# A token-mixing and channel-mixing kernel: ScalarE copies the first block product, and one more query block is computed with seven products

## The chip, the cores and the metric

One core of a Trainium2 chip runs the whole program. TensorE multiplies matrices into PSUM, VectorE and ScalarE do elementwise work and are the ones that read PSUM, GpSimd and SyncE mostly issue DMAs. The engines run side by side and meet through semaphores; each takes its instructions in the order in which the program lists them. The metric is the device time of one execution in microseconds (us).

## The reference

For each of 8 batches, with S = 3008 rows and D = 256 columns:

```python
scores = (1.0 / S) * np.matmul(z, z.transpose(0, 2, 1))
x = u * np.matmul(np.maximum(scores, 0.0) ** 2, v)
xt = x.transpose(0, 2, 1)
h = np.maximum(xt @ w_tok1, 0.0) @ w_tok2
u2 = x + h.transpose(0, 2, 1)
h2 = np.maximum(u2 @ w_ch1, 0.0) @ w_ch2
out = u2 + h2
```

`z` has 64 columns, `w_tok1` is 3008 x 256, `w_ch1` is 256 x 1536 and `w_ch2` is 1536 x 256.

## The kernel before, in words

**Tiling.** A batch is cut into six query blocks of 512 rows (the last has 448), numbered q = 0 to 5; HALF is 3. A batch goes through attention for its six blocks (scores, relu, square, product with v), then the token mixing (`tok1`, `tok2`) and then, block by block, the channel mixing (`ch1`, then `product` or `ch2`). Channel mixing of blocks 3 to 5 of a batch is held back until attention of the next batch is over, so in the steady state TensorE alternates: about 68 us of attention of batch b+1 (267.27 to 335.15 us in the trace for batch 2), then blocks 3 to 5 of batch b together with the token mixing of batch b+1, then blocks 0 to 2 of batch b+1, then attention again. The point where attention ends and the held-back blocks begin is called the handover below.

**Order of work.** The kernel is built by a planner in Python. It keeps an estimated time for each engine, and lists of pieces for TensorE (`heads`, `tails`) with a cost, a list of events that they need and, behind them, operations for ScalarE, VectorE and SyncE (`push`) with a ready time and an estimated duration. It writes the instructions of all engines in the order that it comes to. Once built, the order is fixed.

**Attention's end.** For each of the two column halves of a block, `finish` (L809 on) has ScalarE copy one PSUM bank of the accumulator to a tile `cp` (L825), VectorE adds the other bank (L831) and `gate` multiplies by u into `xT` (L851, and L856 for the last 64 rows). The `cp` tiles come from the pool tag `res`, which has three buffers and is shared with the tiles `u_sb`, which hold a block of u2 until its output is written.

**Channel mixing, first half.** The hidden layer has twelve tiles of 128; `ch1` makes two of them at a time (four matmuls of 512 columns at L1192 into a pair of banks `hp`), and ScalarE, or VectorE where the planner finds ScalarE too busy, evacuates them through a relu (L1231) into `h2pre`. For blocks that are `grouped`, the first four of the twelve tiles (a third) are made another way, as a two by two block product with seven multiplications in place of eight, after Strassen and Winograd. Its seven products are issued in four stages "a" to "d" (`grouped_ch1`, L1312, tile `gp`), of four, four, four and two matmuls of 256 columns. Three sums of inputs (`t_sums`, L1268 to L1278) come first. Between the stages ScalarE copies results within and out of PSUM: after stage a it keeps a copy (L1323) and then forks one bank into the other (L1320); after b it applies a relu (L1327) and forks again; after c VectorE adds both banks with the kept copy (L1338); after d a last relu (L1331). Stage b waits for the first fork, c for the second, d for the two-bank add.

**Channel mixing, second half.** `h2pre @ w_ch2` is also a seven-product block product, for 47 of the 48 blocks. `make_sums` has VectorE form sums of `h2pre` (`hsum`, L1383, L1388, L1401); `product` (L1447) issues the products k = 1 to 7, twelve matmuls of 128 columns each (six for q = 5); `collect` (L1480) has VectorE add each product from PSUM into the output tile `ro`. Products 1, 6, 7, 4 go to the first bank of a pair `xb`, product 2 to the first bank of a pair `zb` and 5 and 3 to its second. VectorE reads product 1 for one quarter of the output, and product 6 then goes on accumulating on top of it in the same bank; product 2 is added to the same quarter by VectorE.

**Orders by hand.** `GROUPED`, `ORDER_LAST` and a plain tuple give, for each block, the order in which its seven products are listed with the pieces of the next block between them: a digit 1 to 7 is a product, 0 is a `ch1` piece of the next block (or a `ch2` piece of the last one), a letter is a stage of the next block's grouped product. `GROUPED` is used where the next block is grouped.

Of the kernel before, what the change touches and what calls it, by code (L numbers as in the profile page):

```python
# [9 lines left out]
F32 = mybir.dt.float32  # L10
BF16 = mybir.dt.bfloat16
# [3 lines left out]
P = 128  # L15
QW = 512
# [42 lines left out]
def kernel(  # L59
# [11 lines left out]
    nc = tc.nc  # L71
    B, S, D = u.shape
# [948 lines left out]

    hid_done = Done()
    BORROW = 3
    GROUPED = ("a", 0, 1, 2, "b", 6, 5, 0, "c", 7, 3, 0, 4, "d")
    VERY_LAST = (B - 1, NQ - 1, CHT // 2 - 1)
    ORDER_LAST = ((1, 2, 6, 5, 7, 0, 3, 4), (1, 2, 6, 5, 0, 7, 3, 0, 4))

    def add_mixer(b):
        st = {}
# [149 lines left out]
        def ch1(q, c2, borrowed, end):  # L1179
            slots = [take_slot()[0] for _ in range(1 + ((b, q, c2) == VERY_LAST))]  # L1180
            W = widths[q]
            xT = xTs[b, q]
            if c2 % 2 == 0:
                live["h2"] += 1
                st["h2", q, c2 // 2] = sb.tile(
                    [P, 4, QW], BF16, tag="h2", name="h2pre", bufs=ROOM["h2"])
            hps = [bank_pair(slot, "hp") for slot in slots]
            hp = hps[0]
            for r in range(2):
                cc = 2 * c2 + r  # L1190
                for dc in range(DT):
                    nc.tensor.matmul(  # L1192
                        hps[r % len(hps)][:, r, :W], w_ch1_sb[:, dc, cc * P:(cc + 1) * P],
                        xT[:, dc, :W], start=(dc == 0), stop=(dc == DT - 1))
# [12 lines left out]

            if (b, q, c2) == VERY_LAST:
                landed, freed = [], Done()

                def evacuate_part(r, t):
                    if r:
                        nc.scalar.activation(h2[:, r, :W], hps[1][:, r, :W], ACT.Relu)
                    else:
                        nc.vector.tensor_single_scalar(h2[:, r, :W], hp[:, r, :W], 0.0, AX.max)
                    landed.append(t)
                    if len(landed) == 2:
                        h2_done[q, c2].t = freed.t = max(landed)
                        keep_ends()

                for r, engine, at, busy in ((0, "dve", end - 0.18, 0.62), (1, "act", end + 0.21, 0.5)):
                    push(engine, at, busy, busy + 0.16, lambda t, r=r: evacuate_part(r, t))
                ring.extend((freed, slot) for slot in slots)
                release("xT", xT_uses[q])
                return
            on_act = load("act") + 0.92 < load("dve") + 2.15

            def evacuate(t):
                recent[0] = h2[:, 0, :1]
                if on_act:  # L1230
                    nc.scalar.activation(h2[:, :, :W], hp[:, :, :W], ACT.Relu)  # L1231
# [22 lines left out]
        g_done = {(q, d, k): Done() for q in range(NQ) for d in range(CHT // 4) for k in range(3)}  # L1254

        def token_quarters(q):

            xT = xTs[b, q]
            quarter = xT.rearrange("p k (m n) -> p k m n", m=2)
            tile_ = {}  # L1260

            def first_two(t):
                live["xT"] += 2
                tile_["T"] = sb.tile(
                    [P, 4, 2 * P], BF16, tag="xT", name="t_sums", bufs=ROOM["xT"])
                st["T", q] = tile_["T"]
                st["s5", q] = sb.tile([P, QW], F32, tag="xT", name="s5", bufs=ROOM["xT"])
# [12 lines left out]
            def begin(t):  # L1280
                push("dve", t, 0.4, 0.53, first_two, room=lambda: live["xT"] < ROOM["xT"] - 1)

            if u_done[q].t is None:
                st["want", q] = begin
            else:
                begin(max(pe[0], u_done[q].t))

        def grouped_ch1(q, d, stage, end):
# [41 lines left out]
            def relu_last(t):  # L1330
                nc.scalar.activation(h[:, 1, 0], half(1), ACT.Relu)  # L1331
                recent[0] = h[:, 1, 0, :1]
                live["xT"] -= 2
                if ("rest", q, d) in st:
                    st.pop(("rest", q, d))(t)

# [77 lines left out]

        def bank_of(q, k):

            if k in (2, 5, 3):
                return st["zb", q][:, int(k != 2)]
            return st["xb", q][:, 0]

        def product(q, k, end):

# [5 lines left out]
            if k == 2:  # L1428
# [28 lines left out]
        def collect(q, k, end):  # L1457
# [9 lines left out]
            def us(m, h):  # L1467
                return st["u", q][:, h, m * n:m * n + n, :]

            blocks_of = {1: (0, 0), 2: (0, 0), 5: (1, 1), 6: (1, 0), 3: (1, 0), 7: (1, 1),  # L1470
                         4: (0, 1)}
            opening = k in (1, 5, 6, 4)

            def add(t):
                if k == 1:
# [26 lines left out]
            if k == 4:  # L1502
                ring.append((done, st["x_slot", q]))

        over = [7] * NQ
# [135 lines left out]
        def add_product(q, k):  # L1641
            needs = {
                1: [Sooner(h2_done[q, c], 0.111 * c) for c in range(CHT // 2)] + w_done[2:],
                2: [], 5: [mix_done, taken[q, 2]], 6: [taken[q, 1]], 3: [taken[q, 5]], 7: [taken[q, 6]],
                4: [taken[q, 7]]}[k]
            kind = {5: 0, 7: 1, 6: 2, 4: 3}.get(k)
            if kind is not None:
                needs = needs + [Sooner(s_done[q, d, kind], 0.222 * d) for d in range(CHT // 4)]
            if q == NQ - 1 and k == 5 and b % 2 == 0:
                needs = needs + [tok1_over[b + 1]]  # L1650
            cost = pairs_of(q) * (CHT // 2) * column_time(P)
            tails.append(Piece(cost, needs, lambda end: product(q, k, end), opens=k == 1,
                               closes=k == 4, key=(b, 2 + q), slot=k in (1, 2),
                               joins=k == 1 and q == NQ - 1))

        added = [0] * (NQ + 1)
# [6 lines left out]
        for q in range(NQ):  # L1663
# [5 lines left out]
            if fast(q):  # L1669
                us_uses[q][0] += bool(rest)  # L1670
                h2_uses[q] += bool(rest)
                for k in (ORDER_LAST[b % 2] if q == NQ - 1 else GROUPED if grouped(q + 1) else
                          (0, 0, 1, 2, 0, 6, 5, 0, 7, 3, 0, 4)):
# [416 lines left out]
```

## Time and profile before

| | us |
|---|---|
| median of 3 runs | 1109.5 (1109.03 to 1110.85) |
| the profiled execution, its own time | 1109.13 |
| its span, first to last instruction | 1107.3 |
| TensorE busy | 1102.2 |
| VectorE busy | 811.5 |
| ScalarE busy | 684.7 |

The granted TensorE clock was full throughout. In lines of the timeline the first number is the start in us from the span's beginning, the second the time from the first start to the last end of the merged instructions, then engine, source line, operation, output and inputs with shapes, and the count; in brackets stands the idle time of the engine just before and what ended it. In lines of groups, the numbers behind the bar are the busy time in us and the mean of one in ns. Lines of waits read: who waited, for whom, us in total, how often, the longest. PEld is TensorE's weight load.

### The profile page before, as it was taken

Reading aid. Unit: us, or ns where it says so; the run is one execution under the profiler, and the core shown is the slowest. Engines: PE = TensorE matmul, PEld = TensorE weight load, DVE = VectorE, ACT = ScalarE, POOL = GpSimd, SP = SyncE. Lnnn points to the kernel's source line nnn. Section 1 sums busy time; section 2 is a strip of 40 time slices with the busy share of each in tenths; the row PEclk is TensorE's granted clock in tenths of the full one; section 3 lists DMA queues with packets and bytes.
Section 4 is the critical chain, followed back from the end, with each engine's and each line's share of the span. In section 5 each row is a group of like instructions: output and inputs, shape, how many; then the busy total and the mean of one; then the engine's idle time right before and its main releaser. Section 6 shows DMA issues by size and latency. Waiting matters only on the chain.

```text
span 1107.3 us, 27459 instructions
## 1 busy us (share of the span) xinstructions
PE 1102.2 (100%) x11199; PEld 695.2 (63%) x11199; DVE 811.5 (73%) x1791; ACT 684.7 (62%) x906; POOL 168.2 (15%) x386
## 2 busy tenths in 40 slices
PE   9999999999999999999999999999999999999998
PEld 3444575776557665576656865557755677556776
DVE  6889865886758866578766796567966778656785
ACT  7999555646854567546665467663776537743464
POOL 5320110321003110032100320003210120000100
PEclk9999999999999999999999999999999999999999
DMA  9999947798978969789896796977989778684222
GB/s 179 167 199 184 149 96 152 127 179 146 190 127 149 190 133 177 127 156 191 140 189 120 133 218 141 170 122 150 198 160 169 116 145 185 125 160 104 64 59 96
DMA packets 465726, 165.55 MB, mean 150 GB/s; under 512 B 433024, under 2 KB 448960, under 8 KB 465600
## 3 DMA queue, kind: packets, MB, share of 16 engines
q1 hardware_dynamic: 436208, 131.11, 58.9%
q0 software_dynamic: 28880, 32.32, 21.5%
q8 instruction: 87, 1.43, 0.6%
q14 instruction: 39, 0.32, 0.1%
q10 hardware_dynamic: 512, 0.38, 0.1%
HBM read 65.40 MB, written 24.64 MB: 81 GB/s over the span
## 4 chain that ended last, share of the span: by engine, by line
PE 99%; DVE 0%; ACT 0%; issue 0%
PE acc L697 42%; PE hp L1192 19%; PE xb L1447 11%; PE zb L1447 8%; PE sc L470 6%; PE h_ps L1128 4%; PE a_ps L1058 3%; PE gp L1312 3%; PE op L1544 2%; PE first_acc L614 1%; PE wp L210 0%; DVE at L516 0%; ACT at L508 0%; DVE zr L183 0%; PE first_acc L189 0%; DVE zT L1850 0%
## 5 line engine op out<-in xcount | busy, mean ns | idle before, releaser
L697 PEld LDWEIGHTS <-v_sb 64*128 64x128 bf16 x4418 | 245.7, 94 | 212.5 <-issue 1.3
L1231 ACT ACTIVATE h2pre<-hp 128x1024 bf16<-128x1024 f32 (+1 forms) x245 | 239.9, 1005 | 182.7 <-PE hp L1192 180.5
L697 PE MATMUL acc<-at,v_sb 64*128 64x512 bf16 (+1 forms) x2738 | 341.6, 374 | 0.0
L508 ACT ACTIVATE at<-sc 128x1024 bf16<-128x1024 f32 (+1 forms) x290 | 286.8, 1027 | 72.0 <-PE sc L470 66.4
L516 DVE TENSOR_TENSOR at<-at 128x1024 bf16<-128x1024 bf16 (+1 forms) x290 | 198.1, 687 | 112.1 <-ACT at L508 107.9
L1192 PE MATMUL hp<-xT,w_ch_sb 128*128 128x512 bf16 (+1 forms) x984 | 238.3, 374 | 0.0
L697 PE MATMUL acc<-fl,v_sb 64*128 64x512 bf16 (+1 forms) x1680 | 193.0, 367 | 0.0
L1192 PEld LDWEIGHTS <-w_ch_sb 128*128 128x128 bf16 x984 | 90.8, 98 | 79.0 <-issue 2.6
L1447 PEld LDWEIGHTS <-hsum 128*128 128x128 bf16 x2088 | 127.9, 98 | 19.6 <-issue 0.5
L470 PE MATMUL sc<-zT 64*128 64x512 bf16 (+1 forms) x732 | 132.4, 359 | 0.1
L1383 DVE TENSOR_TENSOR hsum<-h2pre 128x1024 bf16<-128x1024 bf16 (+1 forms) x141 | 90.0, 647 | 22.7 <-ACT h2pre L1231 12.6
L825 ACT COPY cp<-acc 128x512 f32<-128x512 f32 (+1 forms) x94 | 54.9, 584 | 79.9 <-PE acc L697 69.0
L831 DVE TENSOR_TENSOR cp<-acc,cp 128x512 f32<-128x512 f32 (+1 forms) x94 | 63.4, 675 | 54.8 <-ACT cp L825 54.0
L1447 PEld LDWEIGHTS <-h2pre 128*128 128x128 bf16 x1566 | 93.8, 98 | 10.0
L496 ACT ACTIVATE at<-sc 128x512 bf16<-128x512 f32 (+3 forms) x152 | 56.2, 450 | 29.2 <-PE sc L470 28.8
L1447 PE MATMUL xb<-shared_sb,hsum 128*128 128x128 bf16 x1044 | 73.6, 219 | 0.0
L1480 DVE TENSOR_TENSOR ro<-xb,u_sb 128x256 f32<-128x256 f32 (+1 forms) x141 | 56.3, 400 | 17.9 <-PE xb L1447 17.7
L470 PEld LDWEIGHTS <-zT 64*128 64x128 bf16 x732 | 42.4, 94 | 41.6 <-issue 3.8
L129 POOL CAST mark<-at 128x1 f32<-128x1 bf16 x24 | 9.3, 386 | 388.1 <-DVE at L516 388.1
L851 DVE TENSOR_TENSOR xT<-cp,uT 128x512 bf16<-128x512 f32 (+1 forms) x94 | 62.4, 663 | 0.8
L547 DVE TENSOR_TENSOR at<-at 128x512 bf16<-128x512 bf16 (+3 forms) x152 | 41.0, 320 | 23.8 <-ACT at L496 23.8
L1401 DVE TENSOR_TENSOR hsum<-h2pre,hsum 128x512 bf16<-128x512 bf16 (+1 forms) x141 | 55.1, 400 | 4.1 <-ACT h2pre L1331 2.5
(107 smaller groups left out, 1114.8 us busy)
## 6 DMA issues: line engine op xcount, KB each, us to landing
out_dram<-ro SPq DMA_DIRECT2D x40, 512.0 KB, 3.2
v_sb<-in_v_dram POOLq DMA_DIRECT2D x40, 256.0 KB, 4.6
ur<-in_u_dram POOLq DMA_DIRECT2D x40, 256.0 KB, 5.0
w_tok_sb<-in_moe_w_tok_dram POOLq DMA_DIRECT2D x10, 256.0 KB, 10.5
shared_sb<-in_z_dram POOLq DMA_DIRECT2D x35, 64.0 KB, 4.2
at<-at SPq DMA_TRANSPOSE x114, 2.4
out_dram<-ro SPq DMA_DIRECT2D x7, 256.0 KB, 3.7
fl<-at SPq DMA_TRANSPOSE x105, 4.5
```

Source lines behind the costliest of these rows:

```text
L470: nc.tensor.matmul(sc[:, r, c0:c1], zT[h, k:k + P], zT[h, m + c0:m + c1], start=True, stop=True)
L496: nc.scalar.activation(a3[:, i, c0:c1], sc[:, r, c0:c1], ACT.Relu, scale=inv_S)
L508: nc.scalar.activation(view, sv, ACT.Relu, scale=inv_S)
L516: nc.vector.tensor_mul(view, view, view)
L697: nc.tensor.matmul(o, vs[blk.b, g][rows, i, dh * P:(dh + 1) * P], rhs, start=(dh, h) not in blk.begun, stop=stop, skip_group_check=True)
L831: nc.vector.tensor_add(cp[:, :W], acc[:, 0, :W], cp[:, :W])
L851: nc.vector.tensor_mul(xT[:, dh, :full * P].rearrange("p (t s) -> p t s", s=P), acc[:, :full * P].rearrange("p (t s) -> p t s", s=P), uT[: ...
L1192: nc.tensor.matmul(hps[r % len(hps)][:, r, :W], w_ch1_sb[:, dc, cc * P:(cc + 1) * P], xT[:, dc, :W], start=(dc == 0), stop=(dc == DT - 1))
L1231: nc.scalar.activation(h2[:, :, :W], hp[:, :, :W], ACT.Relu)
L1383: nc.vector.tensor_sub(sums["s"][:, 0:2, :, :n * P], h[:, :, 1], h[:, 0])
L1447: nc.tensor.matmul(to[:, i * P:(i + 1) * P], lhs, weights[:, c2, :], start=(first_use and c2 == 0 and i == 0), stop=(c2 == CHT // 2 - 1), ...
L1480: nc.vector.tensor_add(res(m, h), source, us(m, h) if opening else res(m, h))
```

## The change

1. After product 1, ScalarE copies the first bank of `xb` into the second one (`fork` in `collect`). Product 2 accumulates on that copy, and product 6 on the original. VectorE reads product 1 no more; it takes the quarter once, from the second bank, after product 2, so it does six adds for a block and not seven. Product 2 and product 6 now wait for the copy. `zb` holds 5 and 3 alone and is taken when product 5 comes.
2. Block q = 4 of batches 1 to 6 becomes `grouped` too. Its input sums are started when the fifth `ch1` piece of block 3 is issued (`LATE_T`), and its sums and kept copy live in a buffer of the tag `h2` and not `xT`.
3. The orders are other ones: `GROUPED` is a tuple of orders, by block and apart for the last batch, `PLAIN` is the order where the next block isn't grouped, and `ORDER_LAST` is changed. Products 1 and 2 no longer follow each other; a `ch1` piece, product 6 or a stage stands between.

In the order that is built, the fourth block (q = 3) of batches 1 to 6 begins, right at the handover, with stage a of block 4, product 1, a `ch1` piece and stage b. On ScalarE the copy of the last attention accumulator comes first, then the kept copy and fork of stage a, then the copy of product 1, then the evacuation of the `ch1` piece. In these batches one evacuation each has moved from ScalarE to VectorE.

```diff
-    GROUPED = ("a", 0, 1, 2, "b", 6, 5, 0, "c", 7, 3, 0, 4, "d")
+    LATE_T = 4
+    FIRST = 2
+    GROUPED = (('a', 0, 1, 0, 'b', 6, 2, 5, 'c', 7, 0, 3, 'd', 4), ('a', 0, 1, 0, 'b', 2, 6, 5, 'c', 7, 0, 3, 'd', 4), (0, 'a', 0, 1, 0, 'b', 2, 6, 5, 'c', 7, 0, 3, 'd', 4), ('a', 1, 0, 'b', 2, 5, 6, 'c', 0, 7, 3, 'd', 0, 4), ('a', 0, 1, 0, 'b', 6, 2, 5, 'c', 7, 0, 3, 4, 'd'), ('a', 0, 1, 0, 'b', 6, 2, 5, 'c', 7, 0, 3, 'd', 4), ('a', 0, 1, 0, 'b', 6, 2, 5, 'c', 7, 0, 3, 'd', 4))
+    PLAIN = (0, 1, 0, 5, 2, 6, 0, 0, 7, 3, 0, 4)
-    ORDER_LAST = ((1, 2, 6, 5, 7, 0, 3, 4), (1, 2, 6, 5, 0, 7, 3, 0, 4))
+    ORDER_LAST = ((1, 6, 2, 5, 7, 0, 3, 4), (1, 6, 2, 5, 7, 0, 3, 0, 4))
...
-            if c2 == (3 if q else 0) and q + 1 < NQ and grouped(q + 1):
+            if c2 == (0, 3, 3, LATE_T if b < B - 1 else 3)[min(q, HALF)] and q + 1 < NQ and grouped(q + 1):
                 token_quarters(q + 1)
...
-            return b > 0 and 0 < q <= HALF and d == 0
+            return b > 0 and 0 < q <= HALF + (b < B - 1) and d == 0
...
+                else:
+                    live["h2"] += 1
+                    kept = sb.tile([P, 2, QW], F32, tag="h2", name="t_s5", bufs=ROOM["h2"])
+                    tile_["T"] = kept[:, 0].bitcast(BF16).rearrange("p (k n) -> p k n", k=4)
+                    st["s5", q] = kept[:, 1]
...
-            if k in (2, 5, 3):
-                return st["zb", q][:, int(k != 2)]
-            return st["xb", q][:, 0]
+            if k in (5, 3):
+                return st["zb", q][:, 0]
+            return st["xb", q][:, int(k == 2)]
...
-            first_use = k in (1, 2, 5)
+            first_use = k in (1, 5)
...
+            def fork(t):
+                nc.scalar.copy(bank_of(q, 2)[:, :n * P], bank_of(q, 1)[:, :n * P])
...
             if k == 1:
+                push("act", ready, busy, busy + 0.15, fork, first=2, done=done)
+            elif k == FIRST:
                 with_u(q, ready, lambda at: push(
                     "dve", at, busy, busy + 0.15, add, first=1, room=(home_of(q),),
                     frees=frees_of(q), done=done))
...
-                2: [], 5: [mix_done, taken[q, 2]], 6: [taken[q, 1]], 3: [taken[q, 5]], 7: [taken[q, 6]],
-                4: [taken[q, 7]]}[k]
+                2: [taken[q, 1]], 5: [mix_done], 6: [taken[q, 1]], 3: [taken[q, 5]], 7: [taken[q, 6]],
+                4: [taken[q, 7], taken[q, 2]]}[k]
```

More of the change, by code (lines that the diff above doesn't have):

```diff
@@ L1245, in ch1, with in_xT @@
                 release("xT", xT_uses[q])
-            if c2 == (3 if q else 0) and q + 1 < NQ and grouped(q + 1):
+            if c2 == (0, 3, 3, LATE_T if b < B - 1 else 3)[min(q, HALF)] and q + 1 < NQ and grouped(q + 1):
                 token_quarters(q + 1)
         def grouped(q, d=0):
-            return b > 0 and 0 < q <= HALF and d == 0
+            return b > 0 and 0 < q <= HALF + (b < B - 1) and d == 0
         t_done = {q: Done() for q in range(NQ)}
         g_done = {(q, d, k): Done() for q in range(NQ) for d in range(CHT // 4) for k in range(3)}
+        def in_xT(q):
+            return q <= HALF or b == B - 1
         def token_quarters(q):
@@ L1262, in first_two @@
             def first_two(t):
-                live["xT"] += 2
-                tile_["T"] = sb.tile(
-                    [P, 4, 2 * P], BF16, tag="xT", name="t_sums", bufs=ROOM["xT"])
+                if in_xT(q):
+                    live["xT"] += 2
+                    tile_["T"] = sb.tile(
+                        [P, 4, 2 * P], BF16, tag="xT", name="t_sums", bufs=ROOM["xT"])
+                    st["s5", q] = sb.tile([P, QW], F32, tag="xT", name="s5", bufs=ROOM["xT"])
+                else:
[3 more added lines that the diff above has]
+                    st["s5", q] = kept[:, 1]
                 st["T", q] = tile_["T"]
-                st["s5", q] = sb.tile([P, QW], F32, tag="xT", name="s5", bufs=ROOM["xT"])
                 nc.vector.tensor_sub(tile_["T"][:, 0:2], quarter[:, :, 1], quarter[:, 0])
@@ L1280, in begin @@
             def begin(t):
-                push("dve", t, 0.4, 0.53, first_two, room=lambda: live["xT"] < ROOM["xT"] - 1)
+                push("dve", t, 0.4, 0.53, first_two,
+                     room=(lambda: live["xT"] < ROOM["xT"] - 1) if in_xT(q) else ("h2",))
             if u_done[q].t is None:
@@ L1332, in relu_last @@
                 recent[0] = h[:, 1, 0, :1]
-                live["xT"] -= 2
+                if in_xT(q):
+                    live["xT"] -= 2
+                else:
+                    live["h2"] -= 1
                 if ("rest", q, d) in st:
@@ L1427, in product @@
                 st["xb", q] = bank_pair(st["x_slot", q], "xb")
-            if k == 2:
+            if k == 5:
                 st["z_slot", q], _ = take_slot()
@@ L1468, in us @@
                 return st["u", q][:, h, m * n:m * n + n, :]
-            blocks_of = {1: (0, 0), 2: (0, 0), 5: (1, 1), 6: (1, 0), 3: (1, 0), 7: (1, 1),
-                         4: (0, 1)}
-            opening = k in (1, 5, 6, 4)
+            blocks_of = {2: (0, 0), 5: (1, 1), 6: (1, 0), 3: (1, 0), 7: (1, 1), 4: (0, 1)}
+            opening = k in (2, 5, 6, 4)
+            def fork(t):
+                nc.scalar.copy(bank_of(q, 2)[:, :n * P], bank_of(q, 1)[:, :n * P])
             def add(t):
-                if k == 1:
+                if k == FIRST:
                     home, n_home = take_home(q)
@@ L1503, in collect @@
                 ring.append((done, st["x_slot", q]))
-        over = [7] * NQ
+        over = [6] * NQ
         us_uses = [[1] for _ in range(NQ)]
@@ L1652, in add_product @@
             tails.append(Piece(cost, needs, lambda end: product(q, k, end), opens=k == 1,
-                               closes=k == 4, key=(b, 2 + q), slot=k in (1, 2),
+                               closes=k == 4, key=(b, 2 + q), slot=k in (1, 5),
                                joins=k == 1 and q == NQ - 1))
@@ L1671, in add_mixer @@
                 h2_uses[q] += bool(rest)
-                for k in (ORDER_LAST[b % 2] if q == NQ - 1 else GROUPED if grouped(q + 1) else
-                          (0, 0, 1, 2, 0, 6, 5, 0, 7, 3, 0, 4)):
+                for k in (ORDER_LAST[b % 2] if q == NQ - 1 else GROUPED[q + (b == B - 1) * (HALF + 1)] if grouped(q + 1) else
+                          PLAIN):
                     if isinstance(k, str):
```

## The prediction

> **What bounds the kernel now.** I read the page first, then who waited for whom on TensorE, then the timeline of one handover from attention to channel mixing, engine by engine. The page's first part, its chain, and TensorE's waits:
>
> ```profile
> PE 1102.2 (100%) x11199; PEld 695.2 (63%) x11199; DVE 811.5 (73%) x1791; ACT 684.7 (62%) x906; POOL 168.2 (15%) x386
> PE 99%; DVE 0%; ACT 0%; issue 0%
> PE wp L210 <- DVE zero L1735: 1.2, 1, 1.2
> PE first_acc L614 <- DVE at L516: 0.4, 1, 0.4
> ```
>
> The chain that ended last is TensorE for 99% of the span, and the only waits above 0.15 us on it are two at the start. Busy time alone would not prove a pace, because ends of matmuls are modelled; starts are not. TensorE at the handover of batch 1, where attention ends and mixing begins:
>
> ```profile
> 331.25 3.96 PE L697 MATMUL acc<-fl,v_sb 64*128 64x448 bf16 x40
> 335.15 2.76 PE L1192 MATMUL hp<-xT,w_ch_sb 128*128 128x512 bf16 x12
> 337.75 0.83 PE L1447 MATMUL xb<-w_ch_sb,h2pre 128*128 128x128 bf16 x12
> 338.42 0.83 PE L1447 MATMUL zb<-w_ch_sb,h2pre 128*128 128x128 bf16 x12
> 339.09 1.03 PE L1192 MATMUL hp<-xT,w_ch_sb 128*128 128x512 bf16 x4
> ```
>
> From start to start, twelve 512-column matmuls take 2.60 us (0.217 each), a product of twelve 128-column ones 0.67 us, and nothing lies between. So the time changes by what TensorE must issue, and by any wait that reaches it.
>
> The Trainium skill (Perfetto Trace Analysis, Identifying the Most-Contended Engine) says that matmul busy time is no measure of headroom and that the weight loads' busy share is one. By that share, 63% here, columns would be worth little and the saving below would be 0; the starts above speak for counting them in full, and I do.
>
> **Columns.** The fifth block of batches 1 to 6 swaps two channel pieces of four 512-column matmuls (8 x 0.217 = 1.73 us) for fourteen 256-column ones. The same form in an earlier block:
>
> ```profile
> 239.02 0.38 PE L1312 MATMUL gp<-xT,w_ch_sb 128*128 128x256 bf16 x2
> 239.24 0.38 PE L1312 MATMUL gp<-t_sums,shared_sb 128*128 128x256 bf16 x2
> 239.46 1.03 PE L1192 MATMUL hp<-xT,w_ch_sb 128*128 128x512 bf16 x4
> 240.32 0.83 PE L1447 MATMUL xb<-w_ch_sb,h2pre 128*128 128x128 bf16 x12
> ...
> 240.22 0.61 ACT L1323 COPY s<-gp 128x512 f32<-128x512 f32 x1
> 240.86 0.57 ACT L1320 COPY gp<-gp 128x512 f32<-128x512 f32 x1
> ```
>
> Two take 0.22 us, so fourteen take 1.54. Saved: 0.19 us a block, 6 blocks: **-1.2 us**. The products of the second channel matmul keep their number and columns.
>
> **Work on ScalarE and VectorE.** Forty-seven adds of product 1 on VectorE go and 47 copies on ScalarE come (40 of 256 columns, 7 of 128). The grouped fifth block adds, six times, three sums, one two-bank add, a kept copy, two forks and two relus, and removes two evacuations; six more evacuations move from ScalarE to VectorE.
>
> ```profile
> L1231 ACT ACTIVATE h2pre<-hp 128x1024 bf16<-128x1024 f32 x198 | 198.5, 1026 | 146.7 <-PE hp L1192 145.6 <-issue 1.1
> L1320 ACT COPY gp<-gp 128x512 f32<-128x512 f32 x42 | 23.9, 570 | 1.3
> L1078 ACT COPY a_f<-a_ps 128x128 f32<-128x128 f32 x8 | 2.1, 265 | 33.7 <-PE a_ps L1058 33.7
> L1480 DVE TENSOR_TENSOR ro<-xb,u_sb 128x256 f32<-128x256 f32 x120 | 50.3, 419 | 12.1 <-PE xb L1447 11.9
> ```
>
> No row has a copy of 256 columns from PSUM to PSUM. It lies between 265 and 570 ns; a third of the way, since 256 is a third of the way from 128 to 512, gives an estimate of 0.37 us. ScalarE gains about 40 x 0.37 + 7 x 0.27 = 16.7 us of forks, and the swap of five shorter operations (about 0.58 each) for three evacuations of 1.03 leaves it within 2 us. VectorE loses 47 x 0.42, at most 19.7 us, and gains about as much. Both stay under 75% of the span; these sums cost nothing as long as the queue order holds, which is the next question.
>
> **Does the fork make TensorE wait?** Product 2 (or 6) may start only when the fork is done. In the changed order 1.30 us of other work follows product 1 in grouped blocks (one channel piece 0.86, one pair of short matmuls 0.44), and at least 1.43 (0.76 + 0.67) in the others of full width. The chain is 0.20 us from TensorE to ScalarE (the piece started at 339.09 ends at 339.95, its evacuation starts at 340.15, below), 0.37 for the copy, 0.05 back: 0.62. Alone it is hidden with 0.7 us to spare, so 0 is taken; behind an evacuation that has just begun (0.92 more) it would be 1.54, which bounds the cost at 0.24 us in 27 grouped blocks and 0.11 in 13 plain ones, 7.9 us in all. From below 0 bounds it, since a wait that isn't there can't be removed.
>
> **Waits that go.** Product 6 used to wait for VectorE's add of product 1:
>
> ```profile
> 377.85 0.42 DVE L1480 TENSOR_TENSOR ro<-xb,u_sb 128x256 f32<-128x256 f32 x1
> 378.01 0.38 PE L1312 MATMUL gp<-t_sums,shared_sb 128*128 128x256 bf16 x2
> 378.32 0.83 PE L1447 MATMUL xb<-shared_sb,hsum 128*128 128x128 bf16 x12
> 1092.02 0.92 PE L1192 MATMUL hp<-xT,w_ch_sb 128*128 128x448 bf16 x4
> 1092.50 0.42 DVE L1480 TENSOR_TENSOR ro<-xb,u_sb 128x256 f32<-128x256 f32 x1
> 1092.97 0.83 PE L1447 MATMUL xb<-shared_sb,hsum 128*128 128x128 bf16 x12
> ```
>
> The pair at 378.01 needs 0.22 and the product starts 0.09 late, 0.05 after the add's end; the piece at 1092.02 needs 0.76, the product starts 0.19 late. Both go: **-0.3 us** (0 to -0.3).
>
> **The new wait: six handovers.** In the fourth block of batches 1 to 6 the order now starts with stage a, product 1, one channel piece, stage b. Stage b needs the kept copy and the first fork of stage a, and both stand on ScalarE behind the copy of the last attention accumulator (L825). That copy is late already:
>
> ```profile
> ACT cp L825 <- DVE xT L856: 10.7, 7, 1.7
> 198.34 4.49 PE L1192 MATMUL hp<-xT,w_ch_sb 128*128 128x512 bf16 x20
> 199.63 0.53 ACT L825 COPY cp<-acc 128x448 f32<-128x448 f32 x1 [0.60 <-DVE xT L856]
> ...
> 333.74 0.53 ACT L825 COPY cp<-acc 128x448 f32<-128x448 f32 x1 [1.25 <-PE acc L697]
> 336.01 0.53 ACT L825 COPY cp<-acc 128x448 f32<-128x448 f32 x1 [1.74 <-DVE xT L856]
> 336.44 1.03 ACT L1231 ACTIVATE h2pre<-hp 128x1024 bf16<-128x1024 f32 x1
> ...
> 340.15 1.02 ACT L1231 ACTIVATE h2pre<-hp 128x1024 bf16<-128x1024 f32 x1 [0.85 <-PE hp L1192]
> ...
> 331.55 0.69 DVE L516 TENSOR_TENSOR at<-at 128x1024 bf16<-128x1024 bf16 x1 [3.59 <-ACT at L508]
> 332.16 0.68 DVE L1383 TENSOR_TENSOR hsum<-h2pre 128x1024 bf16<-128x1024 bf16 x1
> 332.76 0.69 DVE L516 TENSOR_TENSOR at<-at 128x1024 bf16<-128x1024 bf16 x1
> 333.36 0.42 DVE L1388 TENSOR_TENSOR hsum<-h2pre,hsum 128x512 bf16<-128x512 bf16 x1
> ...
> 334.37 0.62 DVE L831 TENSOR_TENSOR cp<-acc,cp 128x448 f32<-128x448 f32 x1
> 334.90 0.42 DVE L926 TENSOR_TENSOR d_pair<-x_pair 128x512 bf16<-128x512 bf16 x1
> 335.24 0.55 DVE L851 TENSOR_TENSOR xT<-cp,uT 128x384 bf16<-128x384 f32 x1
> 335.71 0.22 DVE L856 TENSOR_TENSOR xT<-cp,uT 128x64 bf16<-128x64 f32 x1
> ```
>
> Call T the start of mixing, 335.15. The second accumulator's copy needs the buffer of the first, which VectorE frees with L856 at 335.93, so it starts at T+0.86 and the evacuation behind it at T+1.29, though its piece ended at 335.15 + 0.87 = 336.02, ready by 336.22. Before the change nobody needed that evacuation early.
>
> After it, VectorE's queue there reads: square, two sums of 1024, square, a sum of 512, L831, a sum of 512, L851, L856. With the steps above (0.61, 0.60, 0.60, 0.60, 0.34) from 331.55 it is free at T-0.85; the first copy ends at 334.27, so L831 starts at T-0.84, and 0.53 + 0.34 + 0.47 + 0.22 later L856 ends at T+0.72. The copy starts at T+0.80, the kept copy 0.43 later, at T+1.23, the fork 0.64 after that and ends at T+2.44; with 0.05 back stage b can start at T+2.49. TensorE gets there at T + 0.44 + 0.67 + 0.86 = T+1.97. It waits 0.52 us, six times: **+3.1 us**. Behind stage b on TensorE stand all later products, so the delay is not made up. Bounds: 0, if the buffer comes free in time; by the row at 199.63, T+1.29 in batch 0 with the start of mixing at 198.34, the copy is 0.49 later and the wait 1.01, or 6.1 us.
>
> The Trainium skill (PSUM — Partial Sum Buffer, Engine vs sequencer instructions) says that ScalarE's queue is strict first in, first out. By that rule the sum is as above; if the kept copy could pass the waiting one it would start at T+0.64, the fork would end at T+1.85, stage b would be on time and the sum would lack the 3.1. The evacuation held until 336.44 agrees with the rule.
>
> **The sum.** -1.2 - 0.3 + 3.1 = +1.6 us on the profiled execution's own 1109.13 us (span 1107.3, 1.8 around it): **1110.7 us**, 0.11% over the median of the runs shown, 1109.5.
>
> **Rivals.**
> *The handover is on time.* If L856 or the buffer rotation lets the copy start 0.5 us earlier, only -1.5 is left: 1107.6 us. For it speaks that TensorE has no such wait now; against it the seven waits for L856, at every handover.
> *The wait spreads at the handover.* After stage b an evacuation, relu and second fork follow on ScalarE before stage c, which TensorE reaches 2.01 us after b ends. Forks and relu of 0.6 each behind a 1.03 evacuation that starts after the product's fork, at about T+2.65, finish at T+4.9, where stage c is due at T+4.94: nothing to spare. If the copy is 0.3 later than worked out, both waits grow, 6 x (0.3 + 0.1), and the time is 1113.1 us: slower. It decides from a start of the copy at about T+1.0. The batch 0 row speaks for it, the five full steps of VectorE above against it.
> *The fork waits behind evacuations in all 47 blocks*: the 7.9 us above, 1118.6 us. Against it: in the changed order the fork stands ahead of the next evacuation.
> *TensorE's columns are not the limit*: the 1.2 saved counts 0, 1111.9 us. The starts speak against it.
> *The change doesn't do what it says*: matmuls in the changed program are 36 more and columns 3072 fewer in the order built, so I give this nothing beyond the rest.
>
> **Chances.** Forecast 0.47 (its own range 1109.6 to 1111.8), on time 0.23, spread 0.17, forks everywhere 0.06, columns without worth 0.05, the rest 0.02. The range 1107.2 to 1113.1 takes in the first, second and third and leaves out under 2 in 10. About 0.2%, or 2.2 us, is what a measurement of this kernel can tell from no change: faster is below 1107.3, slower above 1111.7. The on-time case sits near the lower bound and gives faster 0.10; spread, forks, half of the columns case and the forecast's upper edge give slower 0.32; the same is left 0.58.
>
> **What would show it.** In the profile after: gp stage b starting about 0.5 us after the piece before it has run out, once in each of batches 1 to 6, released by ScalarE's copy; a copy at L825 released by L856 just ahead; twelve-matmul products at 0.67 us with no wait for the forks elsewhere; hp matmuls 48 fewer and gp 84 more. I am wrong if stage b follows without a gap at the handovers, or if gaps of 0.1 us and more stand before most second products.

## The result, and the profile after

| | us |
|---|---|
| before, median of 12 runs | 1109.27 (1108.88 to 1112.08) |
| after, median of 12 runs | 1111.92 (1111.66 to 1112.44) |
| ratio, 95% interval | 1.0019 [1.0011, 1.0028] |
| forecast | 1110.7 (1107.2 to 1113.1) |
| profiled execution after, its own time and its span | 1112.44, 1110.7 |

The kernel became slower: by 0.19% in the ratio, whose interval leaves out 1, by 2.65 us (0.24%) between the two medians, and by 3.3 us between the two profiled executions. The page after, busy times and chain:

```profile
PE 1101.6 (99%) x11235; PEld 696.2 (63%) x11235; DVE 815.7 (73%) x1774; ACT 694.7 (63%) x965; POOL 173.5 (16%) x386
PE 94%; DVE 2%; ACT 2%; issue 1%; DMA 1%; POOL 0%; ACTq 0%; DVEq 0%
```

Who waited for whom, TensorE's waits above 0.2 us but one at the start, and the one of the accumulator's copy on ScalarE:

```profile
PE gp L1326 <- ACT gp L1334: 2.0, 6, 0.3
PE first_acc L614 <- DMA v_sb<-in_v_dram: 1.4, 1, 1.4
PE xb L1464 <- ACT h2pre L1234: 0.5, 1, 0.5
PE xb L1464 <- DVE ro L1499: 0.4, 1, 0.4
ACT cp L825 <- DVE xT L856: 10.7, 7, 1.7
```

The copy of product 1 on ScalarE, its shortest, median and longest duration in ns:

```profile
L1491 ACT COPY xb<-xb x47: 250/365/432, 140.3 to 1094.6; 128x256 f32<-128x256 f32 x40, 128x128 f32<-128x128 f32 x7
```

TensorE was 99% of the chain and is now 94%. Three waits are new on it: stage b for ScalarE's fork, six times; once product 1 for an evacuation; once a product for VectorE's adds. (The 1.4 for `v_sb` at the start is no part of the change: the same kernel profiled once more shows 0.2 there, and a span of 1109.6.) The seven waits of L825 are to the tenth what they were before.

The handover of batch 1 in the timeline after, TensorE, ScalarE and VectorE; T is 337.68, where attention has ended:

```profile
337.68 0.39 PE L1326 MATMUL gp<-xT,w_ch_sb 128*128 128x256 bf16 x2
...
338.18 0.22 DVE L856 TENSOR_TENSOR xT<-cp,uT 128x64 bf16<-128x64 f32 x1
338.49 0.53 ACT L825 COPY cp<-acc 128x448 f32<-128x448 f32 x1 [1.68 <-DVE xT L856]
338.80 1.03 PE L1195 MATMUL hp<-xT,w_ch_sb 128*128 128x512 bf16 x4
338.92 0.59 ACT L1337 COPY t_s<-gp 128x512 f32<-128x512 f32 x1
...
339.54 0.57 ACT L1334 COPY gp<-gp 128x512 f32<-128x512 f32 x1
...
340.02 0.36 ACT L1491 COPY xb<-xb 128x256 f32<-128x256 f32 x1
340.16 0.38 PE L1326 MATMUL gp<-xT,w_ch_sb 128*128 128x256 bf16 x2 [0.34 <-ACT gp L1334]
...
341.27 0.83 PE L1464 MATMUL zb<-shared_sb,hsum 128*128 128x128 bf16 x12
341.54 0.42 DVE L1499 TENSOR_TENSOR ro<-xb,u_sb 128x256 f32<-128x256 f32 x1
...
341.85 0.57 ACT L1334 COPY gp<-gp 128x512 f32<-128x512 f32 x1
...
342.01 0.83 PE L1464 MATMUL xb<-shared_sb,hsum 128*128 128x128 bf16 x12
...
342.68 0.38 PE L1326 MATMUL gp<-xT,shared_sb 128*128 128x256 bf16 x2
```

The channel piece at 338.80 needs 0.87 us, so stage b was due at 339.67 and starts at 340.16: 0.49 late (the bracket says 0.34, since ends of matmuls are modelled; starts are what counts). The fork before it ended at 340.11. Below, product 6 is due 0.67 after product 5's start, at 341.94, and comes at 342.01, 0.05 after VectorE's add of product 2. Stage c comes at 342.68, on time: its fork ended at 341.85 + 0.57 = 342.42.

Two more places, both in batch 0: first the blocks before attention of batch 1, then the handover:

```profile
162.35 1.03 PE L1195 MATMUL hp<-xT,w_ch_sb 128*128 128x512 bf16 x4
...
162.61 0.42 DVE L1499 TENSOR_TENSOR ro<-xb,u_sb 128x256 f32<-128x256 f32 x1 [1.79 <-PE xb L1464]
...
163.28 0.41 DVE L1499 TENSOR_TENSOR ro<-xb,u_sb 128x256 f32<-128x256 f32 x1
...
163.75 0.83 PE L1464 MATMUL xb<-shared_sb,hsum 128*128 128x128 bf16 x12 [0.37 <-DVE ro L1499]
...
200.74 0.53 ACT L825 COPY cp<-acc 128x448 f32<-128x448 f32 x1 [0.60 <-DVE xT L856]
201.16 3.78 ACT L1234 ACTIVATE h2pre<-hp 128x1024 bf16<-128x1024 f32 x4
...
202.91 0.72 PE L1464 MATMUL xb<-w_ch_sb,h2pre 128*128 128x128 bf16 x10
...
204.08 0.28 PE L1464 MATMUL xb<-w_ch_sb,h2pre 128*128 128x128 bf16 x2 [0.46 <-ACT h2pre L1234]
```

Product 7 was due at 162.35 + 0.87 = 163.22 and waited 0.53 for three adds that stand in a row on VectorE because the first began late. At the handover the evacuations stand behind the late copy of the accumulator; the last two matmuls of product 1 were due at 202.91 + 10 x 0.056 = 203.47 and came 0.61 late. Before the change five channel pieces stood ahead of this product, now four.

The balance of the two profiled executions, from starts alone (for each matmul, the distance to the next start beyond what its columns need at 0.217 us per 512; those above 0.05 us, added up over the trace, are 8.2 us before and 13.1 after):

| where | us |
|---|---|
| columns: 48 hp matmuls less, 84 gp matmuls more (3072 columns at 0.217 per 512) | -1.3 |
| small waits of before that are gone, the two forecast ones (0.29) among them | -0.6 |
| stage b, six handovers | +3.0 |
| product 6 behind VectorE's add of product 2, six times | +0.45 |
| batch 0: product 7, and product 1 at the handover | +1.15 |
| product 5 of the last batch, behind a sum of VectorE | +0.3 |
| the start (+0.6), and the tail behind the last matmul's start (-0.3) | +0.3 |

### The profile page after: what moved, and what is told of

It reads as the page before. It is cut to its first block, busy times and chain, and to the rows that moved or that the text cites. A ratio compares the mean times of both kernels' runs of the same rounds, so it can differ in the third digit from the quotient of the medians.

```text
span 1110.7 us, 27592 instructions
## 1 busy us (share of the span) xinstructions
PE 1101.6 (99%) x11235; PEld 696.2 (63%) x11235; DVE 815.7 (73%) x1774; ACT 694.7 (63%) x965; POOL 173.5 (16%) x386
## 4 chain that ended last, share of the span: by engine, by line
PE 94%; DVE 2%; ACT 2%; issue 1%; DMA 1%; POOL 0%; ACTq 0%; DVEq 0%
PE acc L697 39%; PE hp L1195 17%; PE xb L1464 13%; PE sc L470 6%; PE zb L1464 5%; PE h_ps L1131 4%; PE gp L1326 4%; PE a_ps L1061 3%; PE op L1565 2%; PE first_acc L614 1%; ACT at L508 1%; DVE at L516 1%; DVE hsum L1400 1%; DMA v_sb<-in_v_dram 1%; ACT cp L825 0%
## 5 line engine op out<-in xcount | busy, mean ns | idle before, releaser
L1234 ACT ACTIVATE h2pre<-hp 128x1024 bf16<-128x1024 f32 (+1 forms) x227 | 222.8, 1004 | 170.6 <-PE hp L1195 166.7
L1195 PE MATMUL hp<-xT,w_ch_sb 128*128 128x512 bf16 (+1 forms) x936 | 227.1, 374 | 0.0
L1195 PEld LDWEIGHTS <-w_ch_sb 128*128 128x128 bf16 x936 | 86.4, 98 | 72.3 <-DMA shared_sb<-in_z_dram 0.4
L1464 PEld LDWEIGHTS <-h2pre 128*128 128x128 bf16 x1566 | 97.2, 98 | 14.7 <-ACT h2pre L1234 0.6
L825 ACT COPY cp<-acc 128x512 f32<-128x512 f32 (+1 forms) x94 | 54.9, 584 | 76.0 <-PE acc L697 65.0
L831 DVE TENSOR_TENSOR cp<-acc,cp 128x512 f32<-128x512 f32 (+1 forms) x94 | 63.4, 675 | 50.5 <-ACT cp L825 49.9
L1499 DVE TENSOR_TENSOR ro<-xb,u_sb 128x256 f32<-128x256 f32 (+1 forms) x141 | 54.0, 399 | 35.2 <-PE xb L1464 34.1
L129 POOL CAST mark<-at 128x1 f32<-128x1 bf16 x29 | 11.8, 407 | 410.0 <-DVE at L516 410.0
L1464 PE MATMUL xb<-w_ch_sb,h2pre 128*128 128x128 bf16 x1044 | 74.7, 219 | 0.5 <-ACT h2pre L1234 0.5
L129 POOL CAST mark<-h2pre 128x1 f32<-128x1 bf16 x51 | 26.3, 515 | 213.2 <-ACT h2pre L1234 213.2
```

The source lines that it names most:

```text
L825: nc.scalar.copy(cp[:, :W], acc[:, 1, :W])
L831: nc.vector.tensor_add(cp[:, :W], acc[:, 0, :W], cp[:, :W])
L1195: nc.tensor.matmul(hps[r % len(hps)][:, r, :W], w_ch1_sb[:, dc, cc * P:(cc + 1) * P], xT[:, dc, :W], start=(dc == 0), stop=(dc == DT - 1))
L1464: nc.tensor.matmul(to[:, i * P:(i + 1) * P], lhs, weights[:, c2, :], start=(first_use and c2 == 0 and i == 0), stop=(c2 == CHT // 2 - 1), ...
```

## Experiments

Theory A: the copy of the last attention accumulator (L825) waits for its buffer of tag `res`, ScalarE's queue stands behind it, and that makes the six waits. Rival B: the forks themselves are late, or the wait belongs to VectorE, wherever the copy stands.

**own_room and own_room_before.** The copy gets a place of its own, in the changed kernel and, as a control, in the one before:

```diff
-            cp = sb.tile([P, QW], F32, tag="res", name="cp", bufs=3)
+            cp = zTs[blk.b][:, :8].rearrange("p k n -> p (k n)").bitcast(F32) if (blk.q, dh) == (NQ - 1, 1) else sb.tile([P, QW], F32, tag="res", name="cp", bufs=3)
```

> The changed kernel with one edit: the copy of the last attention accumulator of a batch is written into the batch's own zT tile, whose last reader is done by then, and not into a buffer of tag res. The order of instructions on every engine stays. Theory A (the copy waits for its buffer and ScalarE's queue stands behind it): the copy starts at about T+0.2 instead of T+0.81, the kept copy at T+0.64, stage b is ready by T+1.9 and due at T+1.97, so the six waits of 0.50 us (3.0 in all) go, and batch 0's 0.62 before product 1 with them: 1111.9 - 3.6 = 1108.3 us, or 1107.9 if the six waits of 0.08 before product 6 go too. Rival B (the two forks in a row on ScalarE are what is late, wherever the copy stands): the waits stay above 0.3 us and the time stays at 1111 to 1112.

> The kernel before with the same edit alone, as a control. Theory A: the copy starts about 0.6 us earlier here too, but TensorE waits for nothing behind it, so the time stays at 1109.3 within 0.4 us. If the late copy already cost the kernel before something that I have not seen, it gets faster by up to 0.6 us for each of seven handovers, 1105 us at the least.

Measured: own_room 1108.40 us, 0.9989 [0.998, 0.9998] of before; own_room_before 1109.40, 1.0004 [0.9991, 1.0017]. The same handover in the timeline of own_room, of batch 1:

```profile
336.31 0.39 PE L1326 MATMUL gp<-xT,w_ch_sb 128*128 128x256 bf16 x2
...
336.42 0.53 ACT L825 COPY zT<-acc 128x448 f32<-128x448 f32 x1 [0.98 <-PE acc L697]
...
336.96 0.58 ACT L1337 COPY t_s<-gp 128x512 f32<-128x512 f32 x1
...
337.43 1.03 PE L1195 MATMUL hp<-xT,w_ch_sb 128*128 128x512 bf16 x4
...
337.58 0.57 ACT L1334 COPY gp<-gp 128x512 f32<-128x512 f32 x1
...
338.29 0.38 PE L1326 MATMUL gp<-xT,w_ch_sb 128*128 128x256 bf16 x2
```

The wait of L825 in its rows of waits:

```profile
ACT zT L825 <- PE acc L697: 5.9, 6, 1.0
```

The copy starts at T+0.11, released by the matmuls and no longer by L856; stage b follows its piece by 0.86, without a gap. The six waits and batch 0's 0.61 are gone, the other waits unchanged. With the same two forks, B falls for the handover. In the control the time does not move clear of the noise: in the kernel before, the late copy cost nothing that can be seen. The change is what made it matter.

**late_in_queue.** The buffer stays, only the place in ScalarE's queue changes:

```diff
-        push(engine, end + 0.21, busy, busy + 0.15, copy, first=1)
+        push(engine, end + 0.21 + 0.9 * (blk.b > 1 and (blk.q, dh) == (NQ - 1, 1)), busy, busy + 0.15, copy, first=1)
```

> The changed kernel with the copy of the last attention accumulator (L825) of batches 2 to 7 moved back on ScalarE's queue: behind the kept copy, the fork of stage a and the copy of product 1. TensorE's order stays, and the copy still takes its buffer from res. Theory A (what waits is whatever stands behind that copy in ScalarE's queue): stage b is ready at T+1.9 and its six waits of 0.50 us go; the copy (0.43) now stands ahead of the next evacuation, so the relu and fork of stage b end at about T+4.74 as in the changed kernel, where stage c is due at T+4.5, and six waits of about 0.25 appear there: 1111.9 - 3.0 + 1.5 = 1110.4 us. Rival B (the wait is for the buffer or for VectorE and not for the place in the queue): the waits before stage b stay at 0.4 us or more, 1111.9 us or later.

Measured: 1110.11 us, 1.0005 [0.9987, 1.0022]. The handover (T = 336.71):

```profile
337.35 0.59 ACT L1337 COPY t_s<-gp 128x512 f32<-128x512 f32 x1 [1.52 <-PE gp L1326]
...
337.82 1.03 PE L1195 MATMUL hp<-xT,w_ch_sb 128*128 128x512 bf16 x4
...
338.69 0.38 PE L1326 MATMUL gp<-xT,w_ch_sb 128*128 128x256 bf16 x2
338.72 0.55 ACT L825 COPY cp<-acc 128x448 f32<-128x448 f32 x1
...
339.12 0.83 PE L1464 MATMUL xb<-w_ch_sb,h2pre 128*128 128x128 bf16 x12
...
339.35 0.62 DVE L831 TENSOR_TENSOR cp<-acc,cp 128x448 f32<-128x448 f32 x1
...
340.02 0.83 PE L1464 MATMUL zb<-shared_sb,hsum 128*128 128x128 bf16 x12
```

The kept copy starts at T+0.64 and stage b follows its piece by 0.87, on time: it was the queue. The size of what comes in its place was right, its place was not: not stage c but product 5 waits, 0.23 at 340.02 and 0.19 to 0.30 over the six. What ends just ahead of it is VectorE's L831, at 339.97, which reads the accumulator and is late because the copy is; so product 5 seems to take the accumulator's banks, which the trace does not name.

**fork_alone, fifth_alone, fifth_alone_room.** Each part of the change alone:

```diff
# fork_alone, against after
-            return b > 0 and 0 < q <= HALF + (b < B - 1) and d == 0
+            return b > 0 and 0 < q <= HALF and d == 0
# fifth_alone, against before: grouped, in_xT and LATE_T as after, and for q == HALF
+            ('a', 1, 2, 0, 'b', 6, 5, 'c', 0, 7, 3, 'd', 0, 4)
# fifth_alone_room: that, the copy in zT as in own_room, and for q == HALF
+            ('a', 1, 0, 2, 'b', 5, 6, 'c', 0, 7, 3, 'd', 0, 4)
```

> The changed kernel without its second part: the fifth block of batches 1 to 6 is not grouped, the fork of product 1 and the orders stay (PLAIN for the fourth block). Theory A: the six handover waits (3.0) and the six behind them (0.45) go, the 1.2 us of columns come back, batch 0's two waits (0.53 and 0.62) and the last batch's 0.29 stay: 1111.9 - 3.45 + 1.2 = 1109.7 us, with no wait for a fork above 0.1 us. Rival C (the fork itself costs, product 2 or 6 waiting for ScalarE in many blocks): 1111 to 1114 us with such waits in the trace.

> The kernel before with only the grouped fifth block of batches 1 to 6 and no fork of product 1; the fourth block's order is stage a, product 1, product 2, a channel piece, stage b, so stage b is due at T+2.64 and, by the chain of copies, ready at about T+2.1 to T+2.5. Theory A: no wait there although the copy of the last accumulator is as late as in the changed kernel; only the columns count: 1109.3 - 1.2 = 1108.1 us. Rival D (the grouped fifth block costs by itself at the handover, by its three sums or its place): waits of 0.3 us and more at the six handovers and 1109.5 to 1111 us.

> The kernel before with the grouped fifth block, no copy of product 1, the last accumulator's copy in the batch's zT tile, and the fourth block's order stage a, product 1, piece, product 2, stage b, 6, 5, c. Run fifth_alone lost 0.50 us before the last two matmuls of product 1 (an evacuation behind the late copy) and 0.59 before stage c, six times each. Theory A: with the copy on time the first is 0.2 us or less, and the second, with product 2 moved ahead of stage b, 0.1 or less: 1109.4 - 1.2 = 1108.2 us without any wait, up to 1110.0 with these. Rival D (a grouped fifth block costs by itself): 1112 us or more.

Measured: fork_alone 1110.53 us, 1.0007 [0.9998, 1.0016], where 1109.7 was expected; fifth_alone 1114.01, 1.0038 [1.0025, 1.005], where 1108.1 was expected; fifth_alone_room 1111.13, 1.0006 [0.9987, 1.0025], where at most 1110.0 was expected. In fork_alone no product waits for a fork, so rival C falls. Its rows are batch 0's two waits and one more on VectorE's adds (0.70 us by starts, near 760 us, where the first add waits for an output DMA). By starts, two waits of that kind, 0.13 and 0.15, stand in two other batches; the three are about what the expectation lacked. What went wrong in fifth_alone is in its timeline (attention ends at 334.69):

```profile
334.69 1.04 PE L1193 MATMUL hp<-xT,w_ch_sb 128*128 128x512 bf16 x4
...
335.56 0.53 ACT L825 COPY cp<-acc 128x448 f32<-128x448 f32 x1 [1.74 <-DVE xT L856]
...
335.99 1.03 ACT L1232 ACTIVATE h2pre<-hp 128x1024 bf16<-128x1024 f32 x1
...
337.07 0.28 PE L1462 MATMUL xb<-w_ch_sb,h2pre 128*128 128x128 bf16 x2 [0.35 <-ACT h2pre L1232]
```

and in its rows of waits:

```profile
PE gp L1324 <- ACT gp L1332: 2.6, 6, 0.4
PE xb L1462 <- ACT h2pre L1232: 1.8, 6, 0.3
```

In the order that was built a channel piece stands ahead of stage a, and product 1 needs its evacuation, which stands behind the same late copy: by starts 0.32 to 0.51 us in the six batches. Then stage c waits 0.59 for its fork, which has an evacuation and a relu ahead of it on ScalarE and only two products as cover. So my expectation had looked at stage b alone, and the time is above rival D's 1111 too. In fifth_alone_room the first wait falls to 0.29 and the second is gone, but now product 5 waits 0.24 to 0.30 for VectorE's add of product 2, with which it shares the tile `zb` in the kernel before. The run lists product 5 ahead of 6 behind stage b, where its expectation says 6 ahead of 5, so product 5 came 0.67 us earlier than was thought; the order as written was not run. The 2.9 us between the two runs mix the buffer with the order. Rival D, that a grouped fifth block costs by itself, is not settled here; it falls with six_first below, where the same block runs at the handover without a wait.

**two_pieces.** Stage b later by one channel piece:

```diff
-('a', 1, 0, 'b', 2, 5, 6, 'c', 0, 7, 3, 'd', 0, 4)
+('a', 0, 1, 0, 'b', 2, 5, 6, 'c', 7, 3, 'd', 0, 4)
```

> The changed kernel with the order of the fourth block changed to stage a, piece, product 1, piece, stage b, 2, 5, 6, c, 7, 3, d, piece, 4. Stage b is due at T+2.84, ready at T+2.5 by the late copy: its waits go. But ScalarE's order puts the evacuation of the first piece (0.92) ahead of the copy of product 1, which then starts at T+3.2 and ends at T+3.6, where product 2 is due at T+3.28. Theory A with its chain of copies: six waits of 0.3 to 0.4 us before product 2 take the place of the six of 0.50, none before stage c: 1111.9 - 3.0 + 2.1 = 1111.0 us. If a copy of product 1 behind an evacuation costs nothing: 1108.9. If the handover loses 0.5 us whatever the order: 1111.9.

Measured: 1114.19 us, 1.0038 [1.0021, 1.0055], where 1111.0 was expected. The wait before product 2 is as worked out, 0.35 six times, behind an evacuation on ScalarE:

```profile
339.33 1.03 ACT L1234 ACTIVATE h2pre<-hp 128x1024 bf16<-128x1024 f32 x1
...
340.17 1.75 DVE L926 TENSOR_TENSOR d_pair<-x_pair 128x512 bf16<-128x512 bf16 x5
340.24 0.39 ACT L1491 COPY xb<-xb 128x256 f32<-128x256 f32 x1
...
340.69 0.83 PE L1464 MATMUL xb<-w_ch_sb,h2pre 128*128 128x128 bf16 x12 [0.19 <-ACT xb L1491]
...
341.85 0.41 DVE L1499 TENSOR_TENSOR ro<-xb,u_sb 128x256 f32<-128x256 f32 x1
...
342.31 0.83 PE L1464 MATMUL xb<-shared_sb,hsum 128*128 128x128 bf16 x12
```

The other 3 us were not foreseen. In this batch VectorE takes five sums (L926) ahead of the add of product 2, so the add ends at 342.26 and product 6, due 0.67 after product 5's start at 341.35, is 0.29 late (0.07 to 0.29 over the six); product 7 (0.24) and stage d (0.13) follow, six times each. The delay that ScalarE gave product 2 came back through VectorE's order.

**all_waits_out, six_first, batch0_order, changed_again.** Theory E: readers and writers of the two banks of `xb` wait for each other, as for one tile. In the program as built product 6, in the first bank, does wait for VectorE's add of product 2, which reads the second. Rival F: product 6 waits for its own sums.

```diff
# all_waits_out, against own_room
-    PLAIN = (0, 1, 0, 5, 2, 6, 0, 0, 7, 3, 0, 4)
+    PLAIN = (0, 1, 0, 6, 2, 5, 0, 0, 7, 3, 0, 4)
-    ORDER_LAST = (..., (1, 6, 2, 5, 7, 0, 3, 0, 4))
+    ORDER_LAST = (..., (1, 6, 2, 0, 5, 7, 3, 0, 4))
# all_waits_out and six_first, against own_room
-('a', 1, 0, 'b', 2, 5, 6, 'c', 0, 7, 3, 'd', 0, 4)
+('a', 1, 0, 'b', 6, 2, 5, 'c', 0, 7, 3, 'd', 0, 4)
# batch0_order, against six_first
-                          PLAIN):
+                          (0, 1, 0, 0, 2, 6, 5, 0, 7, 3, 0, 4) if b == 0 else PLAIN):
```

> Run own_room with the orders changed where waits are left: product 6 ahead of 2 in the fourth block of batches 1 to 6 (6, 2, 5) and in PLAIN (0, 1, 0, 6, 2, 5, 0, 0, 7, 3, 0, 4), and a piece ahead of product 5 in the last batch's ORDER_LAST (1, 6, 2, 0, 5, 7, 3, 0, 4). Product 6 waits today for VectorE's add of product 2 although they lie in different banks of one tile xb. Theory E (a reader of one bank holds up a writer of the other, since the two are one tile): with 6 ahead of 2 the six waits of 0.08 (0.47) go, batch 0's 0.53 before product 7 goes, and the last batch's 0.29 at least halves: 1108.4 - 1.2 = 1107.2 us. Rival F (product 6 waits for its sums of h2pre, which are late whatever stands before it): the waits stay or grow, 1108.4 us or more.

> Run own_room with one order changed: product 6 ahead of 2 and 5 in the fourth block of batches 1 to 6. Theory E (readers and writers of the two banks of xb wait for each other as of one tile): the six waits of 0.08 before product 6 go and nothing takes their place at the handover, as in run all_waits_out: 1108.4 - 0.5 = 1107.9 us, batch 0's 0.53 and the last batch's 0.29 stay. The 0.31 before a product 6 near 944 us in all_waits_out may come with this order too (1108.2). Rival F: product 6 waits for its own sums and 0.1 to 0.3 us appears six times, 1109 to 1110 us.

> Run six_first with an order of its own for the plain blocks of batch 0: 0, 1, 0, 0, 2, 6, 5, 0, 7, 3, 0, 4. There the adds of products 2, 5 and 6 stood behind product 6 and product 7 waited 0.53 us for them. With 5 behind 6 the adds of 2 and 6 run under product 5, and the wait shrinks to 0.2 to 0.3 us: 0.25 us less than six_first, 1107.7 us; with two pieces between products 1 and 2 no fork is waited for. If the first add waits for u_sb and not for product 6, the wait stays 0.53 and the time 1107.9.

> The changed kernel unaltered, beside the two runs above on one chip: 1111.9 us, six waits of 0.50 before stage b; if this chip gives another time, the differences are taken within this set. By theory A and E together six_first stands 4.0 us (0.36%) below it.

| run | us | ratio to before |
|---|---|---|
| all_waits_out | 1110.33 | 1.0004 [0.9987, 1.0020] |
| six_first | 1107.91 | 0.9987 [0.9976, 0.9997] |
| batch0_order | 1107.55 | 0.9983 [0.9974, 0.9992] |
| changed_again | 1111.80 | 1.0030 [1.0018, 1.0043] |

The first expectation failed. The six waits before product 6 went, but wherever PLAIN's new order left only one piece between product 1 and product 6, in thirteen blocks, the fork came too late. The timeline of such a block:

```profile
346.20 1.83 ACT L1234 ACTIVATE h2pre<-hp 128x1024 bf16<-128x1024 f32 x2 [0.51 <-PE hp L1195]
...
347.42 0.92 PE L1195 MATMUL hp<-xT,w_ch_sb 128*128 128x448 bf16 x4
...
347.92 0.39 ACT L1491 COPY xb<-xb 128x256 f32<-128x256 f32 x1
...
348.36 0.83 PE L1464 MATMUL xb<-shared_sb,hsum 128*128 128x128 bf16 x12
```

The piece needs 0.76, so product 6 was due at 348.18; the fork, behind an evacuation, ends at 348.31 and the product starts at 348.36: 0.18 late. By starts it is 0.17 or 0.18 ten times in the trace and 0.07 three times. In the last batch, too, it is PLAIN that counts: in its fifth block product 6 now waits 0.57 for a sum on VectorE, where product 5 waited 0.29. The edit of ORDER_LAST does not reach that place. It is taken by the last blocks of batches 1, 3 and 5, and there a product now waits 0.21 that did not before. One more wait, 0.31 near 944 us, stands before product 7 behind a row of VectorE's adds.

six_first keeps only the change at the handover and came out as written. Product 6 starts there right behind stage b, which began its last pair at 338.55 (T is 336.35):

```profile
338.77 0.83 PE L1464 MATMUL xb<-shared_sb,hsum 128*128 128x128 bf16 x12
```

That is earlier than in own_room (340.15) and without a wait, so its sums were not what it waited for: F falls. batch0_order moved batch 0's wait from 0.53 to 0.39 only (0.2 to 0.3 was expected) and the time by 0.36, more than that wait gives and no more than the noise of the runs. Its trace also shows E the other way round: the add of product 2 starts 0.31 us after the start of product 6's last matmul, at 161.96, as it does in the changed kernel at 162.61, although it reads product 2's own bank. It waited for product 6 and not for `u_sb`. What orders the two banks, the way the program is built or the chip, no run tells. batch0_order is 1.7 us faster than the kernel before and, within the same set, 4.25 us faster than the changed one; six_first is 3.9 us faster than that one (4.0 was expected).

## Why the prediction was right

**Columns, -1.2.** Right: 936 matmuls at L1195 for 984, 84 more at L1326. (The rounded 0.19 a block gives 1.14; 3072 columns at 0.217 per 512 give 1.30.) six_first bears the price out: its unneeded distances add up to 8.3 us where those of before are 8.2, and it is 1.3 us faster by the medians; its profiled span is 1.4 us shorter, of which 0.3 lies in the tail behind the last matmul's start, so at least 1.1 is left for the columns. By the weight loads' share alone (the Trainium skill, Perfetto Trace Analysis, Identifying the Most-Contended Engine, which names it beside MFU), 63% in both kernels, columns would be worth little; the trace does not agree, and the rival that priced them at 0 falls, although the time it gave, 1111.9, is the one measured: the missing 1.2 us lay in waits.

**Work on ScalarE and VectorE.** ScalarE's busy time rose by 10.0 us (684.7 to 694.7) and not by about 16.7: the copies of product 1 overlap the operations beside them, 6.7 us in all, and busy time counts an overlap once. VectorE's rose by 4.2, where gain and loss were forecast to be about equal. Neither sum set the time.

**The six handovers, +3.1.** Right, link by link: L856 ended at T+0.72 as worked out, the copy started at T+0.81 (0.80), the kept copy at T+1.24 (1.23), the fork ended at T+2.43 (2.44), stage b started at T+2.48 (2.49). It was due at T+1.99 (1.97); 0.50 us on the mean, 3.0 in all. late_in_queue showed that the place in the queue makes it, as the rule of strict order that the prediction cited says (the Trainium skill, PSUM — Partial Sum Buffer, Engine vs sequencer instructions).

**Stage c on time; forks elsewhere 0.** Right in the changed kernel: the fork ahead of stage c ends at T+4.74, stage c comes at T+5.00, and no product waits for a copy of product 1. The copy takes 0.365, estimated 0.37. The bounds were no idle worry: two_pieces and all_waits_out met the case "behind an evacuation" and paid 0.35 and 0.18.

**Waits that go, -0.3.** Too small. Four others of 0.06 to 0.09 went too, 0.6 in all.

**What the sum lacked, and the step that failed: the list of places.** Three terms, 1.9 us. (1) "Product 6 used to wait for VectorE's add of product 1 ... Both go": it still waits for an add, that of product 2, where 2 stands ahead of 6, and where the add is issued behind product 6, as in batch 0, product 7 waits for all three. (2) I quoted batch 0's late copy as a bound for the six other handovers and did not ask what stands behind it in batch 0 itself, where the new order takes one piece away ahead of product 1. (3) The last batch lost 0.3 at product 5 of its fifth block, which the new order puts ahead of VectorE's sum. With these and the 0.3 more that went, the sum would be -1.3 - 0.6 + 3.0 + 1.9 = +3.0, against 2.65 measured by the medians and 3.3 by the two profiled executions, of which 0.3 lies in the start and the tail. That the time stayed in the range is in part luck: 1111.92, 0.1 us above the forecast's own range, is covered by an upper end that was meant for another case, two growing waits at the handover, which did not come. It is also just above 1111.7, the line that the prediction drew for slower, to which it gave 0.32, against 0.58 for no change.

## What to carry to other kernels

When a new consumer is put behind an operation that was late but unneeded, follow the whole queue from that late operation, in every stage where it occurs, and not only where the diff points. A buffer that nobody waits for in one order may be what everything waits for in the next: here a place of its own for one copy turned 0.2% slower into 0.1% faster. In this program two banks of one tile that different engines read and write were ordered as one, so the order among the products decided whether that cost time.

## What was not expected of the hardware

A cover of one channel piece (0.76 to 0.87 us) is not enough for a copy of 0.37 us on ScalarE when an evacuation may stand ahead of it: from the end of product 1 to the next product it took up to 0.94 us (348.36 less 347.42, in all_waits_out). A profiled execution also carries its own start: the same program had spans of 1110.7 and 1109.6 us, and TensorE's wait of 1.4 us for the DMA of `v_sb` in the one was 0.2 in the other. The 1.1 us between these spans are a third of the 3.3 us between the two profiled executions.
